# One weight load of a decode kernel, cut into nine transfers of unequal row counts

## The chip, the core and the metric

The kernel runs on one core of a Trainium2 chip. The metric is the time of one execution in microseconds (us). Before the change it is 703.93 us, the median of three runs (703.92 to 704.49). A core has 16 DMA engines that bring data from the chip's memory (HBM) into the on-chip buffer of 128 rows (partitions), and five compute and control engines: TensorE (PE), VectorE (DVE), ScalarE (ACT), GpSimd (POOL) and SyncE (SP), which issues the transfers.

## The reference

Two layers are computed, each an attention block with cached keys and values and a gated feed-forward block, for 4 sequences of one new position each. Both layers use the same caches and weights:

```python
x = x + _A_ref(_layernorm(x), k_cache, v_cache, wq, wo)   # 32 query heads, 8 key/value heads, 4096 positions, 128 wide
x = x + _B_ref(_layernorm(x), w1, w3, w2)                 # (silu(x w1) * (x w3)) w2, 512 -> 1792 -> 512
x = x + _A_ref(_layernorm(x), k_cache, v_cache, wq, wo)
x = x + _B_ref(_layernorm(x), w1, w3, w2)
```

Everything is float32. The caches and weights do not fit on the chip, so most of them are read from HBM twice, once for each layer.

## The kernel before

All inputs lie in one HBM array `rows` of 128 rows, in the order in which the first layer uses them. The kernel counts in units of KB, which are 256 floats (1 KB) **in each of the 128 rows**. A load of "24 KB" thus moves 24 KB into each row, 3072 KB in all. The on-chip buffer `space` has room for 218 such units.

`LOADS` (from line 42) is the list of all loads, in the order in which SP issues them. An entry is (source unit, number of units, place in `space`). The function `pump` (line 120) issues the next entry as soon as its place is free; `done` frees a place when the program has passed the last reader of a tile. SP then waits at run time until that reader has really finished. A load is one instruction on SP's queue (line 140; the first one is line 137), and it always covers all 128 rows. There are 88 loads of this kind besides the first one and the store of the result, 90 transfers in all.

A transfer tells that it has landed by a counter. The program has eight of them, `DMAHW0` to `DMAHW7`, and the transfers take them in turn, so that the transfer at place n of SP's queue (from 0) uses counter n mod 8. A transfer is issued only when the one eight places earlier, which used the same counter, has landed in full.

The layers loop over the 8 key/value heads: upwards in layer 0, downwards in layer 1 (`orders`). For a head, `score` (line 322) multiplies the queries with a half of the keys, twice; `exponent` and `turn` make the weights; `weigh` (line 387) multiplies them with the values; and `share_q` (line 295) makes the next head's queries from its tile `wq`. The load that the change touches is `(8, 24, 92)`, place 70 of SP's queue. It brings units 8 to 32 into places 92 to 116: the output weights of head 1 (`wo`, units 8 to 16), the query weights of head 1 (`wq`, 16 to 24) and those of head 0 (`wq`, 24 to 32), for the end of layer 1's attention. Its neighbours in the queue are `(320, 64, 28)` (place 69, the keys of head 2), `(384, 64, 154)` (place 71, the values of head 2) and `(192, 64, 28)` (place 72).

Of the kernel before, what the change touches and what calls it, by code (L numbers as in the profile page):

```python
# [16 lines left out]
P = 128  # L17
# [25 lines left out]
KB = 256  # L43
# [16 lines left out]
    (868, 8, 68), (876, 4, 186), (880, 4, 190), (884, 8, 194), ("stash", 1, 202), (892, 8, 206), ("stash", 0, 214),  # L60
# [5 lines left out]
)  # L66
BUSY = (4, 1, 2)
SCRATCH = 64

# [5 lines left out]
def tile_decode_layers(ctx: ExitStack, tc: tile.TileContext, rows, out):  # L75
    nc = tc.nc
# [9 lines left out]
    def place(at, n):  # L86
        return space[:, at * KB:(at + n) * KB]
# [32 lines left out]
    def pump():  # L120
        while state["next"] < len(LOADS):
            src, n, at = LOADS[state["next"]]
            if src == "stash":
                i, n = n, U // KB
                keys = [("kv", TURN, i)]
                if i == 0 and not state["back"]:
                    return
            else:
                keys = [key for key in stream if src <= offset[key] < src + n]
            if any(taken[at:at + n]):  # L130
                return
            taken[at:at + n] = [True] * n
            if src == "stash":
                for j in range(2):
                    nc.scalar.activation(place(at, n)[:, j * BLOCK:(j + 1) * BLOCK], stored[2 * i + j], AF.Copy)
            elif state["next"] == 0:
                nc.sync.dma_start(space[:, at * KB:], rows[:, 0:n * KB + P])
            else:
                lo = src * KB + (P if src >= LOADS[0][1] else 0)
                nc.sync.dma_start(place(at, n), rows[:, lo:lo + n * KB])  # L140
            for key in keys:
                where[key] = at
                at += size[key[0]]
            state["next"] += 1
# [4 lines left out]
    def done(layer, *key):  # L149
        if layer == 0 and (key[0][:2] == "w1" or key[0] in ("wq", "wo") and key[1] >= HELD or key[:2] == ("kv", TURN) and key[2] in KEPT):  # L150
            return
        at, n = where[key], size[key[0]]
        taken[at:at + n] = [False] * n
        pump()

    pump()


# [40 lines left out]
    def busy(n):  # L199
        if n:  # L200
            pt = scores().rearrange("p (k c) -> p k c", k=KC)
            nc.tensor.matmul(pt[:, 0:n, :], ident, ident.unsqueeze(1).to_broadcast([P, n, P]),  # L202
                             start=True, stop=True)
# [31 lines left out]
    def layernorm():  # L235
        xc, sq = deviation()
        xT = lay_down(xc)
        squares(xc, sq)

        def factor():  # L240
            var = o_ps[1][:, 1:2]
            mean(var, ssq)
            inverse(rstd[:, 0:1], var)

        return xT, factor
# [173 lines left out]
    def turn_o(o, oT):  # L419
        nc.tensor.matmul(misc[:, 0:B * REP], o, head, start=True, stop=True)  # L420
        nc.vector.tensor_copy(oT[:, :, 0:B], misc[:, 0:B * REP].rearrange("p (b h) -> p h b", b=B))  # L421
# [5 lines left out]
    def project_o(layer, g, oT):  # L427
        w = wo_of(g)
        for h in range(REP):
            for k in range(KC):  # L430
                nc.tensor.matmul(x_ps[32 * k:32 * k + B, :], oT[:, h, 0:B], w[:, h, k * P:(k + 1) * P],  # L431
                                 start=(h == 0), stop=(h == REP - 1))
        done(layer, "wo", g)
        nc.vector.scalar_tensor_tensor(x_sb, x_ps, 1.0, x_sb, op0=ALU.mult, op1=ALU.add,
                                       accum_out=rowsum)
# [107 lines left out]
    for layer in range(LAYERS):  # L543
# [13 lines left out]
        for n, (g, (first, last)) in enumerate(order):  # L557
# [7 lines left out]
            if layer and n == 0:  # L565
                state["back"] = True
                pump()
# [22 lines left out]
        nc.scalar.activation(spare, half[:, 0:1], AF.Sigmoid)  # L590
        busy(BUSY[0])
        turn_o(o, oT)
        busy(BUSY[1])
        project_o(layer, g, oT)
        busy(BUSY[2])
        xT, factor = layernorm()
# [50 lines left out]
```

## Time and profile before

| | us |
|---|---|
| median of three runs | 703.93 |
| the profiled execution | 704.12 |
| its span, first to last instruction | 702.3 |
| time around the span | 1.8 |

The profile gives the busy time of each engine, the share of the 16 DMA engines' time in which packets moved, and the chain of work that ended last. Every instruction names its line of the kernel and its output and inputs by tile; `space<-in_rows` is a load. SPq is SP's queue of issues. A view by windows gives the same shares for any stretch of time. The trace also keeps, for each transfer, sixteen marks: the times at which the sixteen shares of it were counted as landed.

### The profile page before, as it was taken

How to read it: one execution, taken by the hardware profiler on the slowest of the kernel's cores; microseconds unless marked ns; L12 is line 12 of the kernel's file. 1: busy time of each engine (PE TensorE's matmuls, PEld its weight loads, DVE VectorE, ACT ScalarE, POOL GpSimd, SP SyncE). 2: the span in 40 equal slices, each digit the busy share in tenths (PEclk: the TensorE clock that was granted, in tenths of full speed). 3: DMA queues.
4: the chain of work that ended last, by engine and by line, in shares of the span. 5: the costliest groups of instructions: out<-in, count | busy, mean ns of one | idle time of the engine just before them, and what ended most of it. 6: DMA issues, size and time to landing. Idle time of an engine off the chain costs nothing.

```text
span 702.3 us, 7502 instructions
## 1 busy us (share of the span) xinstructions
PE 421.3 (60%) x3280; PEld 133.4 (19%) x3280; DVE 144.5 (21%) x512; ACT 41.7 (6%) x100; POOL 3.1 (0%) x10
## 2 busy tenths in 40 slices
PE   1265466644578409667688985744555734567576
PEld 0111121201112103121124221201111211121223
DVE  2012112121023103330231322112120301213221
ACT  0010000100001001000101210000100001000100
POOL 0000000000000000000000000000000000000000
PEclk9997677876769859886999997877877958779999
DMA  9999999999999999999999999999999999999996
GB/s 422 418 415 425 467 419 418 426 457 417 449 414 444 424 438 415 436 423 427 422 418 378 423 430 440 439 438 418 441 440 414 450 419 448 430 425 417 424 425 268
DMA packets 12991, 297.87 MB, mean 424 GB/s; under 512 B 1440, under 2 KB 1568, under 8 KB 4512
## 3 DMA queue, kind: packets, MB, share of 16 engines
q1 hardware_dynamic: 12960, 297.41, 99.0%
q8 instruction: 25, 0.41, 0.2%
q14 instruction: 6, 0.05, 0.0%
HBM read 297.34 MB, written 0.07 MB: 423 GB/s over the span
## 4 chain that ended last, share of the span: by engine, by line
DMA 71%; PE 24%; DVE 1%; another core or an unknown queue 1%; ACT 1%; issue 1%; SPq 0%; ACTq 0%; DVEq 0%
DMA space<-in_rows 71%; PE o L387 10%; PE scores L322 9%; PE sums_ps L306 1%; PE turned L348 1%; ACT p L341 1%; PE scores L202 1%; PE stored L251 1%; DVE acc L335 0%; DVE pT L350 0%; PE o L463 0%; SPq L140 0%; PE sums_ps L431 0%; PE sums_ps L420 0%
## 5 line engine op out<-in xcount | busy, mean ns | idle before, releaser
L322 PE MATMUL scores<-space,qT 128*32 128x512 f32 x1024 | 170.0, 713 | 141.6 <-DMA space<-in_rows 140.8
L387 PE MATMUL o<-space,pT 128*16 128x512 f32 x1024 | 152.8, 710 | 99.3 <-DMA space<-in_rows 91.5
L322 PEld LDWEIGHTS scores<-space,qT 128*32 128x32 f32 x1024 | 36.0, 123 | 218.6 <-issue 180.0
L387 PEld LDWEIGHTS o<-space,pT 128*16 128x16 f32 x1024 | 31.7, 108 | 198.3 <-issue 94.2
L335 DVE TENSOR_REDUCE acc<-scores 128x1 f32<-128x512 f32 x32 | 22.1, 691 | 181.5 <-PE scores L322 181.5
L341 ACT ACTIVATE p<-scores,acc 128x512 f32<-128x512 f32 x30 | 20.6, 687 | 559.0 <-DVE acc L335 432.1
L410 DVE SCALAR_TENSOR_TENSOR o<-o,acc,o 128x128 f32<-128x128 f32 x112 | 39.3, 351 | 49.2 <-PE o L387 45.8
L350 DVE COPY pT<-turned 128x256 f32<-128x256 f32 x32 | 13.6, 425 | 154.3 <-PE turned L348 154.3
L348 PE MATMUL turned<-ident,p 128*128 128x128 f32 x128 | 21.9, 296 | 11.8 <-ACT p L341 11.8
L295 PE MATMUL sums_ps<-space,xT 128*32 128x512 f32 x120 | 22.9, 704 | 2.4 <-DMA space<-in_rows 2.4
L421 DVE COPY o<-sums_ps 128x16 f32<-128x16 f32 x16 | 2.8, 175 | 98.1 <-PE sums_ps L420 98.1
L348 PEld LDWEIGHTS turned<-ident,p 128*128 128x128 f32 x128 | 14.0, 145 | 44.1 <-ACT p L341 25.7
L306 PEld LDWEIGHTS sums_ps<-same,shares 128*128 128x128 f32 x120 | 16.3, 211 | 16.8 <-DVE shares L301 11.1
L306 PE MATMUL sums_ps<-same,shares 128*128 128x4 f32 x120 | 17.6, 270 | 0.9 <-DVE shares L301 0.9
L463 PE MATMUL o<-space,xT 128*32 128x192 f32 (+1 forms) x256 | 13.7, 355 | 3.2 <-DMA space<-in_rows 1.5
L441 PE MATMUL stored<-space,o 128*32 128x512 f32 x104 | 13.5, 592 | 0.0
L301 DVE TENSOR_SCALAR shares<-sums_ps,columns 128x512 f32<-128x512 f32 x15 | 11.1, 743 | 1.7 <-PE sums_ps L295 1.7
L503 PE MATMUL sums_ps<-space,hT 128*4 128x128 f32 x224 | 9.1, 272 | 3.6 <-DMA space<-in_rows 2.9
L211 PE MATMUL o<-columns,same 128*32 128x1 f32 x64 | 2.0, 181 | 14.3 <-DVE columns L548 13.3
L420 PEld LDWEIGHTS sums_ps<-columns,o 128*128 128x128 f32 x32 | 6.1, 239 | 20.6 <-issue 13.0
L463 PEld LDWEIGHTS o<-space,xT 128*32 128x32 f32 x256 | 7.6, 110 | 8.4 <-DVE h L480 2.8
L420 PE MATMUL sums_ps<-columns,o 128*128 128x16 f32 x32 | 7.7, 318 | 0.6 <-DVE o L410 0.6
(101 smaller groups left out, 141.9 us busy)
## 6 DMA issues: line engine op xcount, KB each, us to landing
space<-in_rows SPq DMA_DIRECT2D x11, 4096.0 KB, 21.6
space<-in_rows SPq DMA_DIRECT2D x14, 1024.0 KB, 18.6
space<-in_rows SPq DMA_DIRECT2D x3, 4608.0 KB, 24.6
space<-in_rows SPq DMA_DIRECT2D x2, 6144.0 KB, 30.9
space<-in_rows SPq DMA_DIRECT2D x6, 2048.0 KB, 29.2
space<-in_rows SPq DMA_DIRECT2D x3, 3584.0 KB, 23.5
space<-in_rows SPq DMA_DIRECT2D x2, 5120.0 KB, 28.7
space<-in_rows SPq DMA_DIRECT2D x1, 7680.0 KB, 33.8
```

What stands on the lines that cost most here:

```text
L295: nc.tensor.matmul(wide[32 * k:32 * k + 32, :], xT[:, 32 * k:32 * k + 32], w[:, k, :], start=True, stop=True)
L306: nc.tensor.matmul(misc[:, h * B:(h + 1) * B], shares[:, h * DH:(h + 1) * DH], same[:, 0:B], start=True, stop=True)
L322: nc.tensor.matmul(ps[32 * b:32 * b + 32, :], qT[:, b, at:at + 32], t[:, i * BLOCK:(i + 1) * BLOCK], start=(m < 2), stop=(m >= TILES - 2))
L335: nc.vector.tensor_reduce(acc[:, i:i + 1], ps, axis=AX.X, op=ALU.max, negate=True)
L341: nc.scalar.activation(p.rearrange("p n s -> p (n s)"), ps, AF.Exp, bias=acc[:, i:i + 1], scale=1.0 if scale is None else scale, accum_out ...
L348: nc.tensor.transpose(pt[:, n, :], p[:, n, :], ident)
L350: nc.vector.tensor_copy(pT, pt.rearrange("p n (b r) -> p n b r", b=B)[:, :, :, 0:ROW])
L387: nc.tensor.matmul(o_ps[i][32 * b:32 * b + ROW, :], pT[:, r // 2, b, :], t[:, j * NB * DH:(j + 1) * NB * DH], start=(r < 2), stop=(r >= TI ...
L410: nc.vector.scalar_tensor_tensor(o, o_ps[s][:, j * DH:(j + 1) * DH], acc[:, 16 + NB * s + j:17 + NB * s + j], o, op0=ALU.mult, op1=ALU.add)
L420: nc.tensor.matmul(misc[:, 0:B * REP], o, head, start=True, stop=True)
L441: nc.tensor.matmul(bank[32 * h:32 * h + 32, :], oT[:, h, :], w[:, h, :], start=first, stop=last)
L463: nc.tensor.matmul(bank[32 * j:32 * j + 32, s], xT[:, 32 * k:32 * k + 32], w[:, j], start=(k == 0), stop=(k == KC - 1))
```

## The change

The load `(8, 24, 92)` becomes five entries with the same source units and the same places. The first, of 13 units, is taken in one piece as before. The other four, of 2, 1, 5 and 3 units, are each taken as two transfers, of which the first covers the rows from 0 up to the number in `ROWS` and the second the rest: 100 and 28, 117 and 11, 120 and 8, 126 and 2 rows. The bytes moved and their destination are the same.

```diff
-    (580, 28, 190), (320, 64, 28), (8, 24, 92), (384, 64, 154), ...
+    (580, 28, 190), (320, 64, 28), (8, 13, 92), (21, 2, 105), (23, 1, 107), (24, 5, 108), (29, 3, 113), (384, 64, 154), ...
...
+ROWS = {21: 100, 23: 117, 24: 120, 29: 126}
...
-                nc.sync.dma_start(place(at, n), rows[:, lo:lo + n * KB])
+                for rs in (slice(0, ROWS[src]), slice(ROWS[src], P)) if src in ROWS else (slice(0, P),):
+                    nc.sync.dma_start(place(at, n)[rs], rows[rs, lo:lo + n * KB])
```

SP's queue at this place before, from the load `(580, 28, 190)` to `(192, 64, 28)`. A row gives the rows and the floats per row of a transfer (256 floats are one unit), and the counters for which it waits: those of earlier transfers, and that of PE for readers.

```order
L140 DMA space<-in_rows 128x7168 [waits PE_49]
L140 DMA space<-in_rows 128x16384 [waits DMAHW2_49,PE_49]
L140 DMA space<-in_rows 128x6144 [waits PE_49]
L140 DMA space<-in_rows 128x16384 [waits DMAHW4_49,DMAHW3_49,PE_49]
L140 DMA space<-in_rows 128x16384 [waits DMAHW5_49,DMAHW0_49,PE_49]
```

Here the 24 KB load (128x6144) and `(384, 64, 154)` follow each other, and neither waits for a transfer issued just before.

The same place of SP's queue after the change, from `(320, 64, 28)` to `(192, 64, 28)`. Where a row names no counter that its place would call for, an earlier wait of the queue covers it.

```order
L142 DMA space<-in_rows 128x16384 [waits DMAHW2_49,PE_49]
L142 DMA space<-in_rows 128x3328 [waits PE_49]
L142 DMA space<-in_rows 100x512 [waits PE_49]
L142 DMA space<-in_rows 28x512 [waits DMAHW0_49]
L142 DMA space<-in_rows 117x256
L142 DMA space<-in_rows 11x256
L142 DMA space<-in_rows 120x1280 [waits DMAHW3_49,PE_49]
L142 DMA space<-in_rows 8x1280 [waits DMAHW4_49]
L142 DMA space<-in_rows 126x768 [waits DMAHW5_49,PE_49]
L142 DMA space<-in_rows 2x768 [waits DMAHW6_49]
L142 DMA space<-in_rows 128x16384 [waits DMAHW7_49,PE_49]
L142 DMA space<-in_rows 128x16384 [waits DMAHW0_49,PE_49]
```

One transfer has become nine, so the places behind it move by eight, a full turn of the counters. The row of 126 rows now stands eight places behind `(320, 64, 28)` and waits for its counter, DMAHW5; the row of 2 rows waits for DMAHW6, that of the 13 KB piece; and `(384, 64, 154)` waits for DMAHW7, that of the row of 100 rows.

2 rows, old and new, of the table LOADS are left out of this document.

## The prediction

> **What bounds the kernel now.** I read the page first: span, DMA line, queues, chain.
>
> ```profile
> span 702.3 us, 7502 instructions
> ...
> DMA  9999999999999999999999999999999999999996
> ...
> q1 hardware_dynamic: 12960, 297.41, 99.0%
> q8 instruction: 25, 0.41, 0.2%
> ...
> DMA 71%; PE 24%; DVE 1%; another core or an unknown queue 1%; ACT 1%; issue 1%; SPq 0%; ACTq 0%; DVEq 0%
> ```
>
> The 16 DMA engines are busy from the start to the last slice, 99.0% of the span. The loads are the bound; PE's 24% of the chain lies beside transfers that move meanwhile. So only three things can move the end: the bytes, a gap in which engines have no work, or how evenly the sixteen finish. The bytes stay. For the third I read the last microseconds by windows (the last two columns are the DMA share and GB/s).
>
> ```profile
> 694.00:694.50 0.50, 0.50 (x17) 0.32 (x16) 0.37 (x3) 0.00 (x0) 0.00 (x0) 1.00 1.08 401
> 694.50:695.00 0.50, 0.13 (x8) 0.00 (x0) 0.04 (x1) 0.00 (x0) 0.00 (x0) 1.00 0.75 295
> 695.00:695.50 0.50, 0.23 (x10) 0.22 (x14) 0.00 (x0) 0.00 (x0) 0.00 (x0) 1.00 0.65 242
> 695.50:696.00 0.50, 0.50 (x28) 0.49 (x20) 0.00 (x0) 0.00 (x0) 0.00 (x0) 1.00 0.60 225
> 696.00:696.50 0.50, 0.33 (x13) 0.04 (x4) 0.00 (x0) 0.00 (x0) 0.00 (x0) 1.00 0.51 197
> 696.50:697.00 0.50, 0.39 (x16) 0.36 (x16) 0.00 (x0) 0.00 (x0) 0.00 (x0) 1.00 0.44 172
> 697.00:697.50 0.50, 0.23 (x11) 0.00 (x0) 0.00 (x0) 0.00 (x0) 0.00 (x0) 1.00 0.26 98
> 697.50:698.00 0.50, 0.22 (x9) 0.22 (x13) 0.00 (x0) 0.00 (x0) 0.00 (x0) 1.00 0.20 74
> 698.00:698.50 0.50, 0.40 (x16) 0.11 (x5) 0.00 (x0) 0.00 (x0) 0.00 (x0) 1.00 0.12 45
> 698.50:699.00 0.50, 0.40 (x8) 0.13 (x8) 0.00 (x0) 0.00 (x0) 0.00 (x0) 1.00 0.00 0
> ```
>
> The share falls step by step: the engines finish one after another over 4.5 us, and the program waits for the last. The chain (start, us, what) shows that the last engine counts:
>
> ```profile
> 558.06 41.85 DMA space<-in_rows
> 599.95 5.87 PE o L387 x32
> ...
> 686.24 12.80 DMA space<-in_rows
> 699.08 0.45 PE sums_ps L503 x8
> 699.55 0.29 DVE space L599
> ```
>
> Last load landed 699.04, then 0.45 of PE, 0.29 of DVE and the store. The sixteen landing marks of single transfers, sorted (us; the first mark, then the lags of the others behind it), tell how the spread comes about:
>
> ```
> (320,64,28)  570.26  0.38 0.54 0.88 1.12 1.22 1.28 1.58 1.75 1.89 2.09 2.34 2.69 2.77 2.83 3.00
> (8,24,92)    577.55  0.39 0.56 0.89 1.13 1.24 1.58 1.76 1.90 2.10 2.36 2.69 2.78 2.83 2.83 3.00
> (384,64,154) 596.91  0.39 0.56 0.89 1.14 1.23 1.58 1.76 1.89 2.11 2.35 2.69 2.78 2.83 2.84 3.00
> (64,32,60)   655.03  0.39 0.56 0.90 1.14 1.23 1.77 2.11 2.37 2.69 2.77 2.83 2.84 3.00 3.13 3.44
> (96,32,104)  664.75  0.38 0.56 0.90 1.13 1.24 1.77 2.10 2.37 2.70 2.78 2.83 2.84 3.14 3.46 4.54
> (1234,2,182) 694.56  0.36 0.53 0.85 1.09 1.19 1.72 2.05 2.64 2.71 2.78 3.08 3.39 3.85 4.34 4.47
> ```
>
> Each engine runs at one constant rate; its lag changes only in jumps of about 1.55 us for one engine at a time (3.00 becomes 4.54 between the fourth and fifth row), once for each instruction block of q8. The marks of the last row lie 2.2 behind the first on average, so the last engine ends 4.47 - 2.2 = 2.3 us after the mean: that is what perfect levelling would be worth. And the engine that is 3.00 behind at the changed load is the one, or one of the two, that end the kernel.
>
> **The change, term by term.** First its surroundings:
>
> ```profile
> 549.87 0.33 SPq L140 DMA_DIRECT2D space<-in_rows  x1
> 558.06 0.33 SPq L140 DMA_DIRECT2D space<-in_rows  x1
> 588.09 0.33 SPq L140 DMA_DIRECT2D space<-in_rows  x1
> 573.39 3.64 PE L322 MATMUL scores<-space,qT 128*32 128x512 f32 x16 [15.40 <-DMA space<-in_rows]
> 580.60 1.06 PE L295 MATMUL sums_ps<-space,xT 128*32 128x512 f32 x8 [0.41 <-DMA space<-in_rows]
> space<-in_rows SPq DMA_DIRECT2D x1, 3072.0 KB, 30.7
> L140 SPq DMA_DIRECT2D space<-in_rows x88: 327/328/1182, 1.2 to 686.2; - x88
> ```
>
> The 24 KB load is issued at 549.87 and lands 30.7 later, at 580.6; the load of 320 landed just ahead of 573.39 (its last mark is 573.26). So 24 KB take 580.55 - 573.26 = 7.3 us, **0.302 us per KB** on a full queue. The 64 KB of 384 fit: 599.91 - 580.55 = 19.36.
>
> *Issues.* One becomes nine, 8 x 0.33 = 2.6 us more on SP. SP had 558.06 - 549.87 = 8.2 us to spare here, and the engines stood 20 us deep in queued work: cost nothing, by itself.
>
> *The counters.* This is the added wait. The 13 KB piece and the pieces down to the 8 rows go out in time (from 549.9 on). The 126 rows wait until 320 has landed, 573.3. The 2 rows wait for the 13 KB piece: 573.26 + 13 x 0.302 = 577.2. The load of 384 waits behind them, and for the 100 rows (2 KB, up to 10 rows to an engine, 0.8 us): it is issued at 577.6 to 578.1 **instead of 558.06**. All later loads stand behind it; the next, at 588.09, is released by PE and is not late. What an issue costs on an empty queue is bounded by two rows:
>
> ```profile
> space<-in_rows SPq DMA_DIRECT2D x1, 4160.0 KB, 12.2
> out<-space SPq DMA_DIRECT2D x1, 64.0 KB, 1.5
> ```
>
> The first load of all (32.5 KB a row, 9.8 us at the rate) took 12.2, so 2.4 us until it flowed; the store (0.5 KB a row, 0.15 us) 1.35. I take about 2, nearer to the load, which is the like operation. An engine without work thus starts on 384 at 579.0 to 580.5. In the marks the engines finished the old load between 577.55 and 580.55. So a gap opens for engines that were ahead, and they fall back to about where the slowest was. That costs nothing as long as they don't fall behind it: an idle engine lands 384 at 598.4 to 599.9, against 599.91 for the slowest before. The cover is therefore thin, 0 to 1.5 us, and it is the slowest engine's own work that decides.
>
> *The shares.* Before, each engine took the same of each load: 12960 packets are 90 transfers x 16 x (8 rows + 1 mark). No transfer of before has another row count. If the shares of a transfer stay equal, 100 rows go on 10 engines of 10 rows (no larger number up to 16 divides 100), 28 on 14, 117 on 13, 11 on 11, 120 on 15, 8 on 8, 126 on 14, 2 on 2. If each starts from the same engine, the first two carry 2 x 12 + 1 x 10 + 5 x 9 + 3 x 10 = 109 row-KB of the 11 KB, the next six 106, two 101, then 81, 80, 80, 71, 40 and 0, instead of 88 each. A row-KB is 0.302 / 8 = 0.038 us: ten engines gain 0.5 to 0.8 us of work, six lose 0.3 to 3.3. Were the start moved round, it would lie between this and no change; nothing in the rows tells of that, so I take the fixed start. Small packets add a little: the last 16 row-KB (2 KB, nine packets) took 0.64 us by their last marks (698.39 to 699.03) instead of 0.60; forty packets more on an engine are 0.2.
>
> [...]
>
> *Which engine is the slowest?* The trace doesn't name engines. Ten of sixteen get more, and two engines decide (they end 4.47 and 4.34 behind the first); that both lie among the six that are relieved has a chance of 6/16 x 5/15 = 1 in 8 by count, more if the late ones lie side by side. So I take the case that one of them carries 106 row-KB: 18 x 0.038 + 0.2 = **0.9 us** later, with 384 already in its queue, and nothing behind it changes.
>
> *Readers.* The query weights of head 1 are in the 13, 2 and 1 KB pieces, landed by about 579, ahead of the PE row at 580.60. That gives PE 0.4 us, which it loses waiting for 384 at 599.9.
>
> Sum: 704.12 + 0.9 = 705.0 for an execution like the profiled one, which stands 0.19 above the median; against 703.93 that is **704.8 us**.
>
> **Rivals.**
> *The relieved engines are the slowest ones (faster).* For it: the spread is worth 2.3 us, and one of the six lies 88 row-KB, 3.3 us, lighter. Against it: the late issue of 384. Every engine starts on it at 579.0 at the earliest, and those that still meet a 1.55 us jump end 0 to 1.5 ahead of before. With 2 us for the start: 0.4 less, 703.5.
>
> *Transfers on fewer engines run slower (slower).* Before, every load lays its rows over the engines in one way, and nothing is seen to collide. With 10, 13, 14 or 15 engines on other rows, two may write to one part of the buffer at a time. The price is that the 4.2 us of the pieces on the loaded engines stretch. The nearest row of a slowed packet is q8: 0.2% x 16 x 702.3 / 25 = 0.90 us for 16 KB instead of 0.60, a factor 1.5: 2.1 us more, 706.9. Bounds: factor 1 is the forecast, factor 2 gives 709.0. From a factor of about 1.12 the result is slower by over 0.2%. For it: each engine already runs at a constant top rate. Against it: engines 3 us apart don't write in step.
>
> [...]
>
> *The split does not shift work*, because every transfer is spread over all 16 anyway: then only packets are added, 704.1.
>
> **How the numbers follow.** Forecast 0.42, faster rival 0.22, slower rival 0.28, no shift 0.08. A measurement of this kernel can tell about 0.2%, 1.4 us, from no change. Faster by that needs the shortest start, 1.35 us, and late engines among the relieved: 0.03. Slower by that is nearly all of the slower rival and a little of the forecast: 0.33. The rest, 0.64, lies within. The range reaches from 703.3 (which leaves out the better half of the faster rival) to 707.3 (factor 1.5 and a little; it leaves out a third of the slower one).
>
> **What would show it.** SP's issues: the 126 rows at 573.3, the 2 rows at 577.2, 384 at about 577.9. The q1 packets: with the shares above 12960 - 144 + 144 + 512 rows + 87 marks = 13559; with sixteen marks for each of the eight, 13600. The DMA share of 576 to 580 below that of before. The chain's load of 384 lands at 600.8, and the last at about 700.0. I am wrong if 384 is issued near 558 (then the counters don't hold it), if the end comes before 699.0 (the late engines were relieved), or if it comes after 701 (packets slowed, or engines idled longer than 2.4 us).

## The result: 4 us slower, and the profile after

The change takes **708.03 us** (median of four runs, 707.61 to 708.21) against 704.04 before (four runs in the same round); the ratio is 1.0053 with a 95% interval of 1.0042 to 1.0065. The forecast was 704.8 with a range from 703.3 to 707.3: the sign was right, the size was not, and the time lies outside the range. The profiled execution took 708.17, 4.05 more than that of before.

The page of the changed kernel:

```profile
span 706.2 us, 7518 instructions
...
q1 hardware_dynamic: 13559, 297.41, 99.1%
```

The packets are 13559, the number worked out for equal shares on 10, 14, 13, 11, 15, 8, 14 and 2 engines. The counters show the same: at the landing, 10 marks came for the 100 rows, 14 for the 28, 13 for the 117, 11 for the 11, 15 for the 120, 8 for the 8, 14 for the 126 and 2 for the 2. So the shares were as predicted.

SP's issues of the 126 rows, of the 2 rows and of the load of 384:

```profile
573.26 0.32 SPq L142 DMA_DIRECT2D space<-in_rows  x1
...
578.41 0.23 SPq L142 DMA_DIRECT2D space<-in_rows  x1
...
579.24 0.36 SPq L142 DMA_DIRECT2D space<-in_rows  x1
```

They were expected at 573.3, 577.2 and 577.6 to 578.1. The first is exact; the other two are a little over 1 us late, since the 13 KB piece and the 100 rows, for which they wait, landed later than at the free rate (last marks 578.40 and 579.17). The chain of the changed kernel, at the places that were shown of before:

```profile
579.24 25.10 DMA space<-in_rows
604.38 5.61 PE o L389 x32
...
690.11 12.83 DMA space<-in_rows
702.98 0.45 PE sums_ps L505 x8
703.45 0.29 DVE space L601
```

The load of 384 landed at 604.34 instead of 599.91, **4.4 us later**, and the last load at 702.94 instead of 699.04, 3.9 later. The load of 320 still landed at 573.20 (573.26 before), so everything was lost between 573 and 604. This is the stretch from 575 to 585 by windows, before and then after; the last two columns are the DMA share and GB/s:

```profile
575.00:585.00 10.00, 9.38 (x69) 2.99 (x61) 1.95 (x4) 0.78 (x2) 0.00 (x0) 0.89 1.11 478
```

```profile
575.00:585.00 10.00, 9.47 (x67) 3.14 (x59) 1.95 (x4) 0.78 (x2) 0.00 (x0) 0.86 1.06 269
```

The DMA engines look equally busy (1.11 and 1.06) and move little more than half the bytes. The slow packets counted as busy all the while (1.06 at 269 GB/s, where it was 1.11 at 478 before); only the GB/s beside it shows that the packets themselves became slow. (A packet is counted, with all its bytes, in the window in which it starts, so single windows can pass 1, and 478 is somewhat above the rate at which the bytes moved.) The marks tell which. Sorted, first mark and lags, in the changed kernel:

```
13 KB      574.69  0.29 0.47 0.72 0.91 1.00 1.21 1.35 2.06 2.37 2.92 2.99 3.18 3.52 3.59 3.71
126 rows   582.09  0.24 0.29 0.65 0.81 0.91 1.10 1.22 1.60 1.61 2.12 2.87 2.97 3.04
384        602.42  0.23 0.26 0.31 0.53 0.55 0.60 0.75 0.77 0.82 0.86 1.00 1.33 1.78 1.87 1.91
last load  700.05  0.20 0.27 0.46 0.52 0.55 0.67 0.80 1.74 1.82 1.85 1.87 2.29 2.35 2.54 2.88
```

From the 13 KB piece to the end of the 126 rows it is 7.4 us from first mark to first mark and 6.7 from last to last (the marks don't name the engines), where the shares of the loaded engines are 4.0 us of work at the free rate: a factor of 1.7 to 1.85. In the trace's list of packets, those of 2 KB took 128 ns on average, those of 1 KB 79, of 5 KB 343 and of 3 KB 223. The same sizes on all 128 rows (the run with five loads, further down) took 85, 46, 208 and 124.

### The profile page after: what moved, and what is told of

It is laid out like the page before. It is cut to its first block, busy times and chain, and to the rows that moved or that the text cites. A ratio compares the mean times of both kernels' runs of the same rounds, so it can differ in the third digit from the quotient of the medians.

```text
span 706.2 us, 7518 instructions
## 1 busy us (share of the span) xinstructions
PE 421.9 (60%) x3280; PEld 133.6 (19%) x3280; DVE 144.5 (20%) x512; ACT 41.7 (6%) x100; POOL 3.1 (0%) x10
## 3 DMA queue, kind: packets, MB, share of 16 engines
q1 hardware_dynamic: 13559, 297.41, 99.1%
## 4 chain that ended last, share of the span: by engine, by line
DMA 72%; PE 23%; DVE 1%; another core or an unknown queue 1%; ACT 1%; issue 1%; SPq 0%; ACTq 0%; DVEq 0%
DMA space<-in_rows 72%; PE o L389 9%; PE scores L324 9%; PE sums_ps L308 1%; PE turned L350 1%; ACT p L343 1%; PE scores L204 1%; PE stored L253 1%; DVE acc L337 0%; PE o L465 0%; DVE pT L352 0%; SPq L142 0%; PE sums_ps L433 0%; PE sums_ps L297 0%
## 5 line engine op out<-in xcount | busy, mean ns | idle before, releaser
L324 PE MATMUL scores<-space,qT 128*32 128x512 f32 x1024 | 167.6, 706 | 138.4 <-DMA space<-in_rows 137.7
L422 PEld LDWEIGHTS sums_ps<-columns,o 128*128 128x128 f32 x32 | 6.2, 242 | 20.5 <-issue 12.9
```

The source lines that it names most:

```text
L324: nc.tensor.matmul(ps[32 * b:32 * b + 32, :], qT[:, b, at:at + 32], t[:, i * BLOCK:(i + 1) * BLOCK], start=(m < 2), stop=(m >= TILES - 2))
```

## The experiments

The theory after the result: **collision**. It supposes that a piece cut by rows lays its rows over the engines otherwise than a 128-row load, so that several engines write to one part of the buffer at once, and that their packets slow down for it. The other shares (10 engines of 10 rows for the 100, where 128 rows have 16 of 8) and the slow packets (128 ns against 85 for 2 KB) are measured; that they meet in the buffer no run shows. "Free" below means: at the rate of 128-row loads. The rivals: **late issue** (384 comes out 20 us late and the queue runs dry) and **unequal shares** (only the longer work counts). In the experiments "before" was run beside each: medians 704.13 to 704.29.

### The same nine transfers, cut by columns

```diff
-                for rs in (slice(0, ROWS[src]), slice(ROWS[src], P)) if src in ROWS else (slice(0, P),):
-                    nc.sync.dma_start(place(at, n)[rs], rows[rs, lo:lo + n * KB])
+                w = n * KB
+                cut = ROWS.get(src, P) * w // P
+                for c, d in ((0, cut), (cut, w)):
+                    if c < d:
+                        nc.sync.dma_start(place(at, n)[:, c:d], rows[:, lo + c:lo + d])
```

> The same nine transfers at the same places of the queue and with the same waits, but each pair is cut by columns: all 128 rows, and 100, 117, 120 or 126 of 128 parts of the width first. So every engine takes the same share, on its usual rows. Collision theory (rows spread over the engines in another way than in a 128-row load write to the same part of the buffer and slow down): the slow packets are gone, 704.0 to 705.0. Late-issue theory (the load of 384 comes out at about 578 instead of 558, and the engines run dry): stays near 708. Unequal-shares theory (only the longer work of ten engines counts): 704.0 to 704.6.

Measured: 705.27 us (ten runs), ratio 1.0017 (1.0003 to 1.0032). The chain has the late issue still in it, at 577.67, and the windows of this kernel are nearly back at the old rate:

```profile
577.67 23.04 DMA space<-in_rows
...
686.29 12.88 DMA space<-in_rows
```

```profile
575.00:585.00 10.00, 9.17 (x74) 3.21 (x70) 1.95 (x4) 0.78 (x2) 0.00 (x0) 0.92 1.12 441
```

The bytes, the number of transfers, the waits and the late issue are the same, and most of the loss is gone. So late issue is not the cause; by itself it costs about 1.2 us, with an interval from 0.2 to 2.3. Its marks show what the prediction said of the gap: 384 lands at 599.30 to 600.71, so the engines that were ahead have lost their lead, while the slowest is only 0.8 behind that of before.

### Each piece as two halves of 64 rows

```diff
-ROWS = {21: 100, 23: 117, 24: 120, 29: 126}
+ROWS = {21: 64, 23: 64, 24: 64, 29: 64}
```

> Each of the four pieces is cut into rows 0 to 63 and 64 to 127. Both divide by 16, so the shares are equal, 88 row-KB on each engine; the number of transfers, their bytes and waits are as in the change. Collision theory: 4 rows in a row per engine, two engines on one part of the buffer, packets up to twice as long (3.3 us more work on all sixteen): 706.5 to 708.5. Unequal-shares theory: 704.0 to 704.6. Late-issue theory: near 708, with packets at the usual 84 ns for 2 KB.

Measured: 707.62, ratio 1.0039 (1.0025 to 1.0053). All sixteen marks come for every piece, so the shares are equal, and the loss is nearly that of the change. Unequal shares are not the cause. The 2 KB packets took 132 ns on average, and the rate fell as in the change:

```profile
575.00:585.00 10.00, 10.00 (x66) 2.66 (x58) 1.95 (x4) 0.78 (x2) 0.00 (x0) 0.87 1.08 303
```

### One cut only, with no late issue

```diff
-(8, 13, 92), (21, 2, 105), (23, 1, 107), (24, 5, 108), (29, 3, 113), (384, 64, 154)
+(8, 16, 92), (24, 8, 108), (384, 64, 154)
...
-ROWS = {21: 100, 23: 117, 24: 120, 29: 126}
+ROWS = {24: 64}
```

> The 24 KB load as 16 KB on 128 rows and 8 KB cut into rows 0 to 63 and 64 to 127. Three transfers, so that the load of 384 waits for none of them and is issued near 558 as before. Collision theory alone: 64 row-KB per engine at up to twice the time, 2.4 us more: 705.5 to 706.5. Late-issue theory and unequal-shares theory: 704.0 to 704.3.

Measured: 708.41, ratio 1.0053 (1.0035 to 1.0071). The load of 384 went out at 557.75, and the rate still fell:

```profile
557.75 46.16 DMA space<-in_rows
```

```profile
575.00:585.00 10.00, 9.38 (x74) 3.05 (x67) 1.95 (x4) 0.78 (x2) 0.00 (x0) 0.91 1.10 301
```

Two transfers of 8 KB by halves cost as much as all eight of the change. That is above the 705.5 to 706.5 that were expected from 2.4 us of doubled packets: the 16 KB load ahead of them, on 128 rows, was slowed too (its packets took 699 and 736 ns on average in the kernels with one cut into 126 and 64 rows, 615 in the kernel before).

### Row counts by themselves

A kernel of loads alone, each waiting for the one before, with no PE work and nothing beside it:

```python
for n, r in enumerate((128, 128, 64, 120, 117, 100, 126, 28, 11, 8, 2, 128)):
    nc.sync.dma_start(space[0:r, :], rows[0:r, n * 32 * KB:(n + 1) * 32 * KB])
```

> Leaves out the whole computation: only loads of 32 KB a row, one after the other, each waiting for the one before, with 128, 128, 64, 120, 117, 100, 126, 28, 11, 8, 2 and 128 rows. With equal shares on 16, 16, 16, 15, 13, 10, 14, 14, 11, 8, 2 and 16 engines an engine has 8, 8, 4, 8, 9, 10, 9, 2, 1, 1, 1 and 8 rows, and at 0.0378 us a row-KB plus about 2 us the loads take 11.7, 11.7, 6.8, 11.7, 12.9, 14.1, 12.9, 4.4, 3.2, 3.2, 3.2 and 11.7 us from issue to landing. That is what the unequal-shares theory expects. Collision theory: 64, 120, 117, 100 and 126 rows take clearly longer, up to twice the part above 2 us (64 rows: 9 to 12 us; 120 rows: 15 to 21 us).

Each issue waits for the load before it, so the steps between SP's issues are the times of the loads (from the second 128 rows to the 126 rows):

```profile
13.14 0.33 SPq L82 DMA_DIRECT2D space<-in_rows  x1
25.73 0.52 SPq L82 DMA_DIRECT2D space<-in_rows  x1
38.42 0.41 SPq L82 DMA_DIRECT2D space<-in_rows  x1
60.65 0.31 SPq L82 DMA_DIRECT2D space<-in_rows  x1
74.52 0.28 SPq L82 DMA_DIRECT2D space<-in_rows  x1
98.93 0.32 SPq L82 DMA_DIRECT2D space<-in_rows  x1
112.14 0.32 SPq L82 DMA_DIRECT2D space<-in_rows  x1
```

| rows | engines x rows of one | expected free, us | measured, us |
|---|---|---|---|
| 128 | 16 x 8 | 11.7 | 12.6 |
| 64 | 16 x 4 | 6.8 | 12.7 |
| 120 | 15 x 8 | 11.7 | 22.2 |
| 117 | 13 x 9 | 12.9 | 13.9 |
| 100 | 10 x 10 | 14.1 | 24.4 |
| 126 | 14 x 9 | 12.9 | 13.2 |
| 28 | 14 x 2 | 4.4 | 7.1 |
| 11 | 11 x 1 | 3.2 | 6.4 |
| 8 | 8 x 1 | 3.2 | 6.1 |
| 2 | 2 x 1 | 3.2 | 4.0 |

Half the rows take as long as all of them, by windows at half the rate (second load of 128 rows, then 64, in GB/s in the last column):

```profile
13.20:25.70 12.50, 0.00 (x0) 0.00 (x0) 1.00 0.83 336
25.80:38.40 12.60, 0.00 (x0) 0.00 (x0) 1.00 0.80 166
```

So single transfers with nothing beside them were slowed by their row count: 166 GB/s on 64 rows, 178 on 120 and 135 on 100, against 336 on 128. On 11 and 8 rows, one row an engine, a packet of 32 KB took 3.5 and 3.4 us on average, on 128 rows 1.30. One rival stays untested: every cut changes the rows of `rows` in HBM that are read at one time together with the rows of the buffer that are written, and no run changes one side alone. That the slow part is the buffer's side is therefore the author's supposition, not shown.

Nine rows an engine (126 and 117) were free here (13.2 and 13.9 us, 12.9 expected; 128 rows 12.6, 11.7 expected), which the theory in its simple form took to mean that they are harmless.

### One cut into 126 and 2 rows, and into 120 and 8

```diff
-(8, 13, 92), (21, 2, 105), (23, 1, 107), (24, 5, 108), (29, 3, 113), (384, 64, 154)
+(8, 16, 92), (24, 8, 108), (384, 64, 154)
...
-ROWS = {21: 100, 23: 117, 24: 120, 29: 126}
+ROWS = {24: 126}
```

(and `{24: 120}`).

> 16 KB on 128 rows and 8 KB as 126 and 2 rows. Shares: two engines 9 x 8 + 8 = 80 row-KB, twelve 72, two none, instead of 64 each; 384 is issued near 558. Collision theory: nine consecutive rows per engine took 13.2 us for 32 KB a row in the run of single loads, as fast as free, so nothing slows; only the shares count: 704.0 to 704.9 (8 to 16 row-KB, 0.3 to 0.6 us on the late engine), or down to 703.0 if the late engines are the two without work. If any cut of rows slowed things by itself (more transfers, other row counts), it would be near the 708 of the cut into halves.

> The same with 120 and 8 rows. Shares: eight engines 72 row-KB, seven 64, one none: nearly even, so the unequal-shares theory gives 704.0 to 704.4. Collision theory: 120 rows took 22 us for 32 KB a row instead of 12 in the run of single loads, so 64 row-KB cost 2.4 us more on fifteen engines, and the 8 rows about 1 more: 706.5 to 708.5.

Measured: 126 and 2 rows 709.36, ratio 1.0070 (1.0054 to 1.0087); 120 and 8 rows 708.57, 1.0059 (1.0044 to 1.0074). The second lies at the upper edge of what the collision theory said (708.5). **The first is a miss**: the cut that was free alone cost no less than the others. The window of the kernel with 126 rows:

```profile
575.00:585.00 10.00, 9.24 (x67) 2.87 (x59) 1.95 (x4) 0.78 (x2) 0.00 (x0) 0.88 1.11 270
```

Its 8 KB packets took 625 ns on average, twice the 314 of such packets in the kernel before. So a layout that was free alone (13.2 us for 32 KB a row) was slowed in the kernel's full queue. Two explanations were left: that it is enough for the engines to be out of step, or that it takes other loads beside it.

### Out of step, or beside other loads

First, again without the computation, loads of 12, 8 and 4 rows that set the engines apart, with 32 KB a row behind them:

```python
for g, r in enumerate((128, 126, 117, 120)):
    for j, s in enumerate((12, 8, 4)):
        load(s, 32 * g + 8 * j, 8)       # rows, place, KB
    load(r, 32 * g + 32, 32)
```

> Leaves out the whole computation: four times, three small loads (12, 8 and 4 rows of 8 KB) that set the sixteen engines 0.3 to 2 us apart, with a load of 32 KB a row queued right behind, of 128, 126, 117 and 120 rows in turn. The cut with 126 rows was as fast as free when loaded alone, with all engines in step, and yet the 8 KB with 126 rows in the kernel ran at half rate. Refined collision theory (rows off an engine's usual place meet their usual owner or each other as soon as the engines are out of step): 128 rows stay at 1.21 us a packet of 32 KB, 126 and 117 rows rise to 1.4 to 2.2 on average. If step does not matter and 126 rows are slow only beside other loads: 126 and 117 stay at 1.21.

Measured: 128, 126 and 117 rows stay at 1.21 to 1.22 us a packet after the first one, and 120 rows take 2.57. This does not decide it: the engines stood only about 1 us apart (the second packets of the 128 rows start between 17.72 and 18.63), less than one of these packets.

So, with packets of 8 KB, and in a second part with 126 rows between two 128-row loads that are in flight at the same time:

```python
for g, r in enumerate((128, 126, 117, 64)):
    load(12, 32 + 16 * (g % 2), 16); load(8, 0, 16); load(4, 16, 16)
    load(r, 32 + 16 * ((g + 1) % 2), 8)
for r in (128, 126):
    load(128, 32, 16); load(r, 64, 8); load(128, 72, 20); load(128, 32, 8)
```

> Leaves out the whole computation. First four times three loads of 12, 8 and 4 rows (16 KB a row) that set the engines apart by 1 to 3 us, which is three to ten packets of 8 KB, and right behind them 8 KB a row on 128, 126, 117 and 64 rows. Then twice a queue of 16 KB on 128 rows, 8 KB on 128 rows (the second time on 126), and 20 KB on 128 rows, all in flight. A packet of 8 KB takes 0.31 us when free. Theory that being out of step by more than a packet is enough: the 126 and 117 rows behind the spread engines take 0.4 to 0.6 us a packet, the 128 rows 0.31. Theory that it takes other loads beside them: those stay near 0.31, and only the 126 rows between two 128-row loads rise to 0.4 to 0.6, with the packets of 20 KB (0.76 free) of the two engines that have no share of the 126 rows slowed too. If neither, all stay at 0.31, and the half rate in the kernel is not explained.

The first part is spoiled: the spreading loads are slow themselves (their packets of 16 KB took 1.7 to 1.8 us on average), and even the 128 rows behind them took 695 ns a packet on average. The second part is clean. Between 128-row loads, the 8 KB on 128 rows took 309 ns in every packet, and the 20 KB packets behind them 761. With 126 rows in the middle, their packets took 504 on average (up to 845), and the 20 KB packets on 128 rows 862 on average (up to 1681). From SP's first issue of such a group

```profile
54.24 0.36 SPq L84 DMA_DIRECT2D space<-in_rows  x1
...
72.72 0.33 SPq L84 DMA_DIRECT2D space<-in_rows  x1
```

to the last mark of the 20 KB (70.23 and 91.45) it is 16.0 us with 128 rows and 18.7 with 126: **2.7 us for one piece of 8 KB**, of which 0.3 are the ninth row of a share. This is one execution of each group. Beside 128-row loads, a cut that was free alone was slowed (504 ns against 309), and the ordinary load behind it was slowed too (862 against 761). Whether being out of step is enough without other loads stays open.

### The change without its late issue

```diff
-(24, 5, 108), (29, 3, 113), (384, 64, 154)
+(24, 5, 108), (384, 64, 154), (29, 3, 113)
```

> The change with the load of 384 put ahead of the pair of 126 and 2 rows, so that it waits only for the load of 320 and is issued at 573.3, some 5 us before any engine could run dry; the cut by rows is as in the change. Collision theory: the pieces stay slow (1.5 to 1.75 times) and so does the result, 707.0 to 708.5. Late-issue theory: the gap is gone, 704.0 to 705.5.

Measured: **711.78**, ratio 1.0105 (1.0086 to 1.0123). Both theories missed, the late-issue theory on the wrong side. SP's issue of 384 and its landing stand in the chain:

```profile
575.05 31.49 DMA space<-in_rows
```

Its marks spread from 600.25 to 606.54, and those of the last load over 6.3 us, against 2.9 in the change.

Not all of this comes from the new order. In the traced execution (710.96) the load of 320, ahead of all pieces, landed at 574.99 instead of 573.20, after a delay that grew between 378 and 399 us, in loads that the two kernels have in common. The traced execution of the halves has such a delay of 0.9 us, so it is not peculiar to this order. Counted from the landing of 320, the last load comes 130.89 us later here, 129.74 in the change and 125.77 before. So the loss behind 320 is 5.1 us, 1.15 more than in the change, and not the 3.7 that the medians suggest. Whether the other three executions had the delay too is not known. That the late issue shields the load of 384 from the pieces would explain the 1.15, but is not shown: by the packets' starts only one engine went on to 384 early (576.80), the other fifteen from 580.89 on, and the 3 KB piece now lies between two 128-row loads, which may cost as well.

### All rows, five loads

```diff
-ROWS = {21: 100, 23: 117, 24: 120, 29: 126}
+ROWS = {}
```

> The five loads of 13, 2, 1, 5 and 3 KB, each on all 128 rows: five transfers instead of one, no cut by rows, and 384 is issued near 558 as before. Collision theory and late-issue theory: nothing is left that costs, 703.9 to 704.5. If small or many transfers cost by themselves, 1 us or more above before.

Measured: 704.47, ratio 1.0001 (0.9991 to 1.0010): no difference. The rate stays up:

```profile
575.00:585.00 10.00, 9.17 (x62) 2.60 (x54) 1.95 (x4) 0.78 (x2) 0.00 (x0) 0.78 1.13 470
```

Cutting the load by units costs nothing that these runs can tell.

### Which engines are late

Seven tiny loads behind 384 in the kernel before, with 15 to 9 rows in one kernel and 8 to 2 in the other:

```diff
+                if src == 384 and LOADS[state["next"] - 1][0] == 8:
+                    for j, r in enumerate((15, 14, 13, 12, 11, 10, 9)):
+                        nc.sync.dma_start(probe[0:r, 2 * j:2 * j + 2], rows[0:r, 2 * j:2 * j + 2])
```

> The kernel before with seven tiny loads of 15, 14, 13, 12, 11, 10 and 9 rows (8 bytes a row, into a spare tile) queued behind the load of 384. By equal shares they use 15 to 9 engines; their marks come behind the load's own mark of the same engine, so the lag that is missing from the 15 marks is that of the sixteenth engine, and so on down to the tenth. It names the engines, not a cost. If the late engines (2.6 to 3.0 us behind the first at this load) are among the six that the change relieves, they are missing from the marks of the 10 rows; if they carry more in the change, they are still there. The end is later than before by one to three us, since the next loads wait for a place in the turn of counters (the load of 192 at about 600 instead of 588).

> The same with tiny loads of 8, 7, 6, 5, 4, 3 and 2 rows, which name engines 7 down to 0 by the marks that go missing. Late engines that the change loads most (the first eight) show up here; otherwise the marks of the 8 rows hold only the smaller lags. The end as in the probe of the high engines.

They ended at 707.93 and 707.08, 3.8 and 3.0 us above before, where one to three were expected. From each row count to the next smaller one, exactly one lag goes missing from the marks. Counted so that the one missing at 15 rows is the sixteenth, those of the sixteenth down to the tenth engine are, in the first execution, 0.96, 2.4, 2.5, 1.6, 2.6, 1.5 and 1.5 us, and the slowest, 2.7, is still there among the first nine. In the second, the eighth down to the fourth are 0.5, 2.6, 2.5, 1.1 and 1.8; the seventh is one of the two slowest, and the other is among the upper eight. The late engines are thus scattered over both halves, and the lags differ between the two executions.

## Why the prediction was wrong

- *The bound and the spread*: right. The end is the last landing plus 0.45 and 0.29 us of PE and DVE, as before.
- *The shares*: right, by 13559 packets and by the marks. 100 rows went on 10 engines, 28 and 126 on 14, 117 on 13, 11 on 11, 120 on 15, 8 on 8 and 2 on 2, and in the halves 64 on 16. The fixed start was an assumption; the probes fit it, since each smaller row count, from 15 to 9 in one kernel and from 8 to 2 in the other, drops one more engine of the same set.
- *The rate of a share*: **this is the step that failed.** "A row-KB is 0.302 / 8 = 0.038 us" was taken from 128-row loads and used for other row counts. (24 KB in 7.3 us are 0.304 a KB; 0.302 is the figure of the 64 KB load. That changes nothing.) It measured 0.064 to 0.070 for the loaded engines (6.7 to 7.4 us for 106 row-KB). The slower rival named the slow packets, with too small a price (whether they meet, and where, in the buffer or in HBM, no run shows): a factor of 1.5 where 1.7 to 1.85 was measured, and nothing for the neighbours (the 13 KB piece, whose packets took 545 ns on average instead of 502, and the first packets of 384, which took up to 4.37 us instead of 2.42). Its chance of 0.28 rested on "engines 3 us apart don't write in step" as a reason against it; the kernel with one cut into 126 rows shows that engines 2.5 us and more apart (the spread of its marks at 320), with other loads beside them, were slowed (625 ns against 314 for 8 KB).
- *The sum*: on the slowest engine, 0.9 us of longer shares was foreseen and 4.4 measured at 384, so 3.5 are left for the slow packets. Equal shares (the halves) lost nearly as much, so that the forecast had the right sign for a reason that carries little of the loss: that was luck. Of the 4.4, 0.5 were given back: the later jumps of 1.55 us met engines that were not last (the spread grew from 1.91 to 2.88, before from 3.00 to 4.47). That leaves the 3.9 at the end.
- *The counters and the late issue*: right as an event (573.26, and 384 near 579 instead of 558), and right that it costs little by itself (1.0017 with the columns).
- *The start on an empty queue*: not refuted. "About 2", between 1.35 and 2.4, was taken. With the columns, the first mark of 384 (599.30) less 19.35 of work is 2.3 us after the issue at 577.67. The later marks, up to 600.71, tell less: the last mark of the pieces came at 581.04, so some engines were still at work when 384 was issued.
- *Which engine is late*: the case taken, that a late engine carries more, is what the probes make likely. In neither execution are both of the slowest engines among the six that are relieved. No version that beats both kernels came out of this.

## What to carry to other kernels

In this kernel, which is bound by its loads, the rate held while every transfer covered all 128 rows (from 575 to 585 us 478 GB/s before, 470 with five loads, 441 with the columns). A cut by rows, even the one that was free alone, broke this for the piece and for the loads beside it (269 to 326 GB/s): 8 KB a row cut in two cost 4 to 5 us, more than the 2.3 us that perfect levelling could have brought. Cut by units, which cost nothing (1.0001), or by columns (1.0017, with the late issue in it), and read the GB/s beside the DMA share, since the engines with slow packets looked busy here (1.06 at 269 GB/s).

## What the runs showed of the hardware that was not expected

- A single load of 64 rows took as long as one of 128 (12.7 and 12.6 us for 32 KB a row), and 120 rows took 22.2; 126 rows took 13.2.
- Packets of an ordinary 128-row load were slowed beside a neighbour on 126 rows: 20 KB in 862 ns on average and up to 1681, instead of 761.
- Engines that were ahead lost their lead when the next load was issued late: with the columns the spread of the marks fell from 2.48 us, at the last piece, to 1.41 at 384.
